# First attention: half of the mask copies moved behind v copies on VectorE, w_v loaded by column halves, output products of the early tiles one step later

## The chip, the cores and the metric

The kernel runs on one core of one Trainium2 chip. The metric is the device time of one execution in microseconds (us), lower is better. An execution is called fast when it is within 1.5% of the fastest one of its kernel; every execution quoted here was fast, except one that was run only once (its state is unknown, and it is marked).

Engines are named as in the profile: PE is TensorE's matrix unit, PEld its weight loads, DVE is VectorE, ACT is ScalarE, POOL is GpSimd, SP is SyncE (in these kernels it only issues transfers, 373 of them in the trace before). A name such as `QK<-stg` reads "output from input". `L433` is a line of the kernel before.

## The reference

Two layers, A and B, run twice in the order A, B, A, B, each added to a residual. Only the first A is touched. It is an attention over a window of 8 positions with a stride of 2:

```python
def _A_ref(x, wqkv, wo):                 # x: (1, 2048, 576), already normalized
    B, S, D = x.shape; H = 32; Dh = D // H          # 18 values per head
    W, dil = (8, 2)
    q, k, v = ...(x @ wqkv)...                      # each (B, H, S, Dh)
    idx = pos[:, None] - (jnp.arange(W) * dil)[None, :]
    mask = idx >= 0
    logits = einsum('bhsd,bhswd->bhsw', q, kg) * scale
    logits = where(mask, logits, -1e9)
    attn = softmax(logits)
    o = einsum('bhsw,bhswd->bhsd', attn, vg)
    return o.transpose(...).reshape(B, S, D) @ wo
...
x = A_x
x = x + _A_ref(_layernorm(x), A_wqkv, A_wo)
x = x + _B_ref(_layernorm(x), ...)
x = x + _A_ref(_layernorm(x), A_wqkv, A_wo)
x = x + _B_ref(_layernorm(x), ...)
```

## The kernel before

q and k of all heads lie in one tile `QK`. A head takes 18 partitions of a group of 32; the other 14 hold a pattern that adds the window mask inside the score product itself. DVE copies that pattern into `QK`, one half of the positions at a time. These are the mask copies, eight of them in two groups of four:

```python
def fill_window_rows(self, QK, half):
    ...
    c0 = PADL + half * n
    for g0 in (0, 4):
        for a in range(2):
            nc.vector.tensor_copy(out=QK[:, a, g0:g0 + 4, c0:c0 + n]...,
                                  in_=self.pat[:, a, None, None, PADL:PADL + 256].to_broadcast(...))
```

A q or k product (`PG`) is made by PE, copied to a staging tile `stg` (some staging space is borrowed from `win2a`, so the profile calls it `QK<-win2a`), and then moved into its partitions of `QK` by small transfers, issued in turn by POOL and SP:

```python
def PG(d, qk, cc, dve, queues=(nc.sync, nc.gpsimd)):
    ...
    for c in range(5):
        nc.tensor.matmul(pp[:, :], lhsT=w, rhs=self.xnT[...], start=(c == 0), stop=(c == 4))
    evac(stg[:, qk, gi * 512:(gi + 1) * 512], pp[:, :], dve)      # dve: on DVE, else on ACT
    ...
    for dst, src in moves:
        dma_rr[0] += 1
        self.dma(dst, src, eng=queues[dma_rr[0] % len(queues)])
```

The front, in its order (v products are `VW`, normalizations `R_` and `A_`):

```python
self.load_wv(nc.sync)
...
rows[1]()                       # mask rows, on DVE and POOL
setup_bufs(nc.gpsimd)
...
VW(1, 0, False)
VW(1, 1, False)
...
rows[2](nc.scalar)              # stores the mask rows, issued by ACT
...
self.fill_window_rows(QK, 0)    # first group of mask copies
...
for k_, (d, cc) in enumerate(order):
    for qk in ((1, 0) if d < 4 else (0,)):
        PG(d, qk, cc, False, ...)
    ...
    if k_ == 6:
        R_(12, 4)
        A_(12, 13, 14, 15)
        self.fill_window_rows(QK, 1)        # second group
T_(12, 13, 14, 15)
...
for t in range(nvw0, nvw):                  # v products of tiles 4 to 7
    for hh in range(2):
        VW(t, hh, False)                    # copied by ACT
```

Then come 38 steps, two for each of 19 attention tiles. A step multiplies scores (`L_ps`), takes the exponential (`P_sb`), multiplies with v (`O_ps`), writes `o_t`, and fills the rest with q, k and v products. After a tile's second step SP issues a transpose of `o_t` to `oT`, and some steps later the output product (`pw<-oT`) of a block of 128 rows uses it:

```python
for i in range(NS):
    t = -(-(i + 1) * P // QT) - 1           # last attention tile that block i needs
    s = 2 * t + (6 if li == 0 and i == 0 else 5 if t < NT - 5 else 4 if t < NT - 3 else 3)
    at(s - 5, XO, i)                        # SP loads the residual
    at(s, WO, i, 0)                         # output product, two halves
    at(s + 1, WO, i, 1)
    ...
    if i < NS - 1:
        at(s + 4, LN_T, i)                  # SP transposes the normalized rows
...
L_mm(0)
EXP(0)
for d, qk, cc in pre:                       # six more q/k products
    PG(d, qk, cc, True, q2)
for s in range(NST):
    if s + 1 < NST:
        L_mm(s + 1)
        EXP(s + 1)
    PV(s)
    for f, a in table.pop(s, []):
        f(*a)
```

The softmax here doesn't subtract the row's maximum and nothing guards it: scores larger than these inputs give would overflow.

Of the kernel before, what the change touches and what calls it, by code (L numbers as in the profile page):

```python
# [18 lines left out]
P = 128  # L19
D = 576  # L20
# [42 lines left out]
class K:  # L63
# [51 lines left out]
    def build_window_rows(self, c):  # L115
# [6 lines left out]
        nc = self.nc  # L122
        R = c.tile([P, 2, MR, 16], bf16, name="win_rows")
        self.pat = self.consts.tile([P, 2, 272], bf16, name="win_pat")
# [7 lines left out]
        nc.gpsimd.iota(n[:], pattern=[[1, 3]], base=15, channel_multiplier=1)  # L132
        nc.gpsimd.memset(R[:, 0, 0:8, :], half)
        nc.gpsimd.affine_select(out=R[:, 0, 0:8, :], in_=R[:, 0, 0:8, :], compare_op=ALU.is_ge, fill=-half,
                                base=1, pattern=[[2, 8], [-1, 16]], channel_multiplier=0)
        nc.gpsimd.memset(R[:, 1, 0:8, :], 0.0)
        for off in (2, 3):
# [152 lines left out]
            self.dma(R["wqk"][:, :, w0:w0 + n], self.A_wqkv[0:512, c0:c0 + n].rearrange("(c p) n -> p c n", p=P), eng=eng)  # L290
            self.dma(R["wqk4"][:64, w0:w0 + n], self.A_wqkv[512:576, c0:c0 + n], eng=eng)

    def load_wv(self, eng):
        R = self.right
        self.dma(R["wv"][:, 0:4, :], self.A_wqkv[0:512, 2 * D:3 * D].rearrange("(c p) n -> p c n", p=P), eng=eng)
        self.dma(R["wv"][:64, 4, :], self.A_wqkv[512:576, 2 * D:3 * D], eng=eng)

    def load_wo(self, eng):
        R = self.right
# [20 lines left out]
    def layer_A(self, li):  # L320
        nc, tc, cfg = self.nc, self.tc, self.cfg
        S, NT, XW, NS = cfg.S, cfg.NT, cfg.XW, cfg.NS
# [6 lines left out]
        QK = main.tile([P, 2, 8, XW], bf16, name="QK")  # L329
# [13 lines left out]
        R = self.right  # L343
# [7 lines left out]
        def tdim(t):  # L351
            nq = min(QT, S - QT * t)
            return HALO + nq, nq


        def setup_bufs(eng):
            for pb in P_bufs:
                eng.memset(pb[:, :, :, QT:P], 0.0)
            for ob_ in o_bufs:
                eng.memset(ob_[:, D:640], 0.0)  # L360
# [10 lines left out]
        def VW(t, hh, dve):  # L371
            nk = tdim(t)[0]
            pv = self.PT_tile([P, 512], f32, "pv")
            for c in range(5):
                nc.tensor.matmul(pv[:nk, 0:288], lhsT=self.xnT[:, c, QT * t:QT * t + nk],  # L375
                                 rhs=wv_sb[:, c, hh * 288:(hh + 1) * 288], start=(c == 0), stop=(c == 4))
            evac(v_ext[:nk, t, 16 * hh:16 * hh + 16, 0:DH], pv[:nk, 0:288].rearrange("p (b d) -> p b d", d=DH), dve)
# [4 lines left out]
        def PG(d, qk, cc, dve, queues=(nc.sync, nc.gpsimd)):  # L382

            cb, gi = divmod(cc, CBW // 512)
            key = (d, cb)
            if key not in stg_tiles:
                if cb == 0 and d >= 3 and lent:
                    stg_tiles[key] = lent[d - 3]
                else:
                    stg_tiles[key] = stgs[stg_rr[0] % NSTG]  # L390
                    stg_rr[0] += 1
                stg_left[key] = (2 if d < 4 else 1) * (CBW // 512)
            stg = stg_tiles[key]
            pp = self.PT_tile([P, 512], f32, "pp")
            w0 = d * P + (640 if qk else 0)
            for c in range(5):
                w = wqk[:, c, w0:w0 + P] if c < 4 else wqk4[:, w0:w0 + P]
                nc.tensor.matmul(pp[:, :], lhsT=w, rhs=self.xnT[:, c, PADL + cc * 512:PADL + (cc + 1) * 512],  # L398
                                 start=(c == 0), stop=(c == 4))
            evac(stg[:, qk, gi * 512:(gi + 1) * 512], pp[:, :], dve)  # L400
            stg_left[key] -= 1
            if stg_left[key] == 0:
                stg_tiles.pop(key)
                cs = slice(PADL + cb * CBW, PADL + (cb + 1) * CBW)
                moves = []
                for h in range(d * P // DH, H):
                    a, b = max(h * DH, d * P), min((h + 1) * DH, (d + 1) * P)
                    if a >= b:
                        break
                    g, rg = divmod(h, 4)  # L410
                    q0, s0, n = 32 * rg + a - h * DH, a - d * P, b - a
                    if d < 4:
                        moves.append((QK[q0:q0 + n, :, g, cs], stg[s0:s0 + n, :, :]))
                    else:
                        for a_ in range(2):
                            moves.append((QK[q0:q0 + n, a_, g, cs], stg[64 * a_ + s0:64 * a_ + s0 + n, 0, :]))
# [3 lines that stand above are left out]
# [85 lines left out]
        q2 = (nc.gpsimd, nc.sync, nc.gpsimd)  # L505


        if li == 0:
# [3 lines left out]
            def x_load(xg, i0, n, eng):  # L512
                self.dma(xg, self.A_x[i0 * P:(i0 + n) * P, :].rearrange("(i p) d -> p i d", p=P), eng=eng)
                for k_ in range(n):
                    xts[i0 + k_] = xg[:, k_, :]
# [2 lines left out]
            x_load(x0[:, 0:1, :], 0, 1, nc.sync)  # L518
            x_load(x0[:, 1:2, :], 1, 1, nc.scalar)
            x_load(x0[:, 2:4, :], 2, 2, nc.sync)  # L520
            self.load_wv(nc.sync)
            x_load(x1[:, 0:4, :], 4, 4, nc.sync)
            self.load_wqk(nc.sync)
            x_load(spare, 8, 4, nc.sync)
# [6 lines left out]
            rows = self.build_window_rows(sb)  # L531
# [5 lines left out]
            def S_(*tiles):  # L537
                for i in tiles:
                    st = sb.tile([P, 2, nc.vector.BN_STATS_DIM], f32, name="ln_st", tag="ln_st", bufs=3)
                    for s in range(2):  # L540
                        nc.vector.bn_stats(out=st[:, s, :], in_=xts[i][:, s * 288:(s + 1) * 288])
                    nc.vector.bn_aggr(out=mvs[:, i, :], in_=st[:])
# [4 lines left out]
            def R_(i0, n):  # L547
                nc.gpsimd.tensor_tensor(out=rstds[:, i0:i0 + n], in0=rstds[:, i0:i0 + n],
                                        in1=self.neg_half[:, 0:1].to_broadcast([P, n]), op=ALU.pow)
            xns = {}  # L550

            def A_(*tiles):
                for i in tiles:
                    xns[i] = xn = self.xn_bufs[self.xn_rr % len(self.xn_bufs)]
                    self.xn_rr += 1
                    nc.vector.tensor_scalar(out=xn[:, 0:D], in0=xts[i], scalar1=mvs[:, i, 0:1],
                                            scalar2=rstds[:, i:i + 1], op0=ALU.subtract, op1=ALU.mult)

            def T_pe(i):
                xn = xns.pop(i)  # L560
                pt = self.PT_tile([P, 5, P], bf16, "pt")
                for c in range(5):
                    nc.tensor.transpose(pt[:, c, :], xn[:, c * P:(c + 1) * P], self.ident[:])
                r = PADL + i * P
                nc.scalar.copy(out=self.xnT[:, :, r:r + P], in_=pt[:])  # L565
# [7 lines left out]
            S_(1)  # L573
            E_(1, 1)
            R_(1, 1)
            rows[1]()
            setup_bufs(nc.gpsimd)
            A_(0)
            T_pe(0)
            VW(0, 0, False)  # L580
            VW(0, 1, False)
            A_(1)
            T_pe(1)
            VW(1, 0, False)
            VW(1, 1, False)
            S_(2, 3)
            E_(2, 2)
            R_(2, 2)
            rows[2](nc.scalar)
            A_(2, 3)  # L590
            T_pe(2)
            T_pe(3)
            x_load(sb.tile([P, 4, D], bf16, name="x_in3", tag="x_in", bufs=2)[:], 12, 4, nc.sync)
            S_(4, 5)
            E_(4, 2)
# [23 lines left out]
            for k_, (d, cc) in enumerate(order):  # L619
                for qk in ((1, 0) if d < 4 else (0,)):  # L620
                    PG(d, qk, cc, False, (nc.gpsimd, nc.sync) if d in (0, 4) else q2)
                if k_ == 3:
                    VW(3, 0, False)
                    VW(3, 1, False)
                if k_ == 6:
                    R_(12, 4)
                    A_(12, 13, 14, 15)
                    self.fill_window_rows(QK, 1)
            T_(12, 13, 14, 15)
            nvw0, nvw = 4, 8  # L630
        else:
# [12 lines left out]
            nvw0, nvw = 0, 4  # L644
        for t in range(nvw0, nvw):
            for hh in range(2):
                VW(t, hh, False)

        pieces = []

# [18 lines left out]
                at(2 * t - 2 + hh, VW, t, hh, 2 * t - 2 + hh >= PG_END and hh == 0)  # L669
        for i in range(NS):  # L670
            t = -(-(i + 1) * P // QT) - 1
            s = 2 * t + (6 if li == 0 and i == 0 else 5 if t < NT - 5 else 4 if t < NT - 3 else 3)
            at(s - 5, XO, i)
            at(s, WO, i, 0)
            at(s + 1, WO, i, 1)
            at(s + 1, LN_STATS, i)
            at(s + 2, LN_XN, i)
            at(s + 2, XST, i)
            if i < NS - 1:
                at(s + 4, LN_T, i)  # L680
# [9 lines left out]
        L_mm(0)  # L690
        EXP(0)
        for d, qk, cc in pre:
            PG(d, qk, cc, True, q2)
        for s in range(NST):
            if s + 1 < NST:
                L_mm(s + 1)
# [343 lines left out]
```

## Time and profile before

The kernel took 1200.14 us (median of 3 executions, 1200.07 to 1201.12). One execution was profiled; its span was 1197.5 us.

| what | value | view |
|---|---|---|
| PE busy | 1182.4 us, 99% | page, part 1 |
| first attention ends (end of its last output product) | 141.93 us | trace |
| stall 1: PE waits for q and k in `QK`, until 50.9 us | 3.3 us | waits of PE |
| half clock after it | 6.8 us | windows |
| stall 2: an output product waits for a transpose, until 95.0 us | 2.0 us | waits of PE |
| half clock after it | 3.4 us | windows |

The page of the kernel before. Part 1 is the busy time of each engine, part 2 cuts the span into 40 slices of about 30 us and gives tenths, and part 4 is the chain of waits that ended last.

```profile
span 1197.5 us, 20773 instructions
...
PE 1182.4 (99%) x8554; PEld 621.5 (52%) x8554; DVE 545.3 (46%) x1200; ACT 378.1 (32%) x599; POOL 277.9 (23%) x382
...
PEclk9899999999999999999999999999999999999999
...
PE 96%; DMA 2%; ACT 1%; issue 0%; POOL 0%; SPq 0%; DVE 0%; ACTq 0%; POOLq 0%
```

PE is busy nearly always, so a change can win only where PE stands still or runs slowly. One slice, the second (30 to 60 us), has a clock digit below 9.

The waits of PE in the kernel before: what was waited for, total us, number of times, longest.

```profile
PE L_ps L433 <- DMA QK<-win2a: 3.3, 2, 3.1
...
PE pw L487 <- DMA oT<-o_t: 2.0, 1, 2.0
...
PE pv L375 <- ACT xnT L565: 1.5, 2, 0.8
```

The first line is stall 1, the second stall 2, the third a wait in the front. Next, stretches of the trace before (windows view): bounds in us, then the busy us of each engine with its number of instructions, then the granted PE clock (1.00 is full), the share of the DMA engines' time, and GB/s. A DMA share above 1 (1.19 in the first line) means that the packets' times, added up, are more than the time of the 16 engines in that stretch, so packets overlap.

```profile
47.20:50.60 3.40, 0.36 (x8) 0.26 (x8) 0.48 (x1) 0.00 (x0) 0.07 (x1) 1.00 1.19 165
...
50.60:57.40 6.80, 6.60 (x80) 2.85 (x76) 2.23 (x6) 3.45 (x4) 0.00 (x0) 0.50 0.28 86
...
90.00:95.00 5.00, 3.03 (x61) 2.12 (x57) 3.29 (x11) 3.51 (x5) 4.72 (x5) 1.00 1.18 151
95.00:98.40 3.40, 3.38 (x42) 2.09 (x43) 1.17 (x3) 1.39 (x2) 3.31 (x5) 0.50 0.97 271
```

In the 3.40 us of stall 1 PE is busy for 0.36 us. After it PE is busy (6.60 of 6.80 us) but at half its clock, and after stall 2 again, for 3.4 us. What does half a clock cost? Here is a piece of the chain of waits before (start, duration, what), first at half clock, then at full:

```profile
51.85 2.14 PE pp L398 x5
53.99 0.51 PE L_ps L433 x16
54.51 0.53 PE O_ps L453 x16
...
58.15 1.09 PE pp L398 x5
...
59.88 0.50 PE O_ps L453 x16
```

Five q/k products take twice as long, but sixteen small `O_ps` products hardly longer (0.53 against 0.50 us), and sixteen score products take 0.51 us, within the 0.33 to 0.65 us that they take at full clock. So such a stretch costs less than half of its length. By an estimate from these differences it is about 2.2 us for the 6.83 us after stall 1, and about 1.2 us for the 3.41 us after stall 2 (five output products took 1.38 us there against 0.78, five v products 1.17 against 0.63). Stall 1 thus costs about 3.3 + 2.2 us, stall 2 about 2.0 + 1.2 us. Below, a half-clock window is 3.41 us of such a stretch.

Why are q and k late? Here is the timeline before, for POOL and DVE: start, duration, engine, line, operation.

```profile
39.13 4.88 POOL L77 DMA_DIRECT2D QK<-win2a  x1
...
39.28 4.63 DVE L197 COPY QK<-win_pat 128x4096 bf16<-128x4096 bf16 x4
...
44.01 3.26 POOL L77 DMA_DIRECT2D QK<-win2a  x6
```

One issue on POOL takes 4.88 us, where its neighbours take about 0.55 us. It begins 0.15 us before the second group of mask copies and ends 0.1 us after it. Six more issues follow it. The chain of waits before, taken from 36 to 52 us, passes through these issues and the landing of one of them (start, duration, what):

```profile
44.01 2.26 POOL QK L77 x4
46.27 4.55 DMA QK<-win2a
...
50.87 0.46 PE L_ps L433 x2
```

That the copies hold the issue is read from these times: it ends 0.1 us after the copies, as the first of POOL's moves does after the first group (1.56 us, ending 0.1 us after copies from 24.0 to 28.6 us), and the semaphore that it waits for had been complete since 38.32 us, so that wait was over. In the same stretch SP issued two moves from 40.81 us on in 1.45 us.

### The profile page before, as it was taken

The page shows a single profiled execution, that of the slowest core. Times are in us where ns is not written, and L with a number is a line of the kernel's source. Part 1 is how long each engine was busy: PE and PEld are TensorE (multiplying, and loading weights), DVE is VectorE, ACT ScalarE, POOL GpSimd, SP SyncE. Part 2 cuts the span into 40 slices and gives each one's busy share as a digit, 9 for nine tenths or more (in the row PEclk, how much of TensorE's full clock was granted, in tenths as well). Part 3 has the DMA queues.
Part 4 walks back from the last instruction along what each step waited for, and adds up shares of the span by engine and source line. Part 5 has one row for each costly group of instructions (what it writes and reads, how often), then busy time and mean ns, then how long its engine had stood idle before and what let it go on. Part 6 is the DMA issues. An engine that isn't in the chain of part 4 may idle for free.

```text
span 1197.5 us, 20773 instructions
## 1 busy us (share of the span) xinstructions
PE 1182.4 (99%) x8554; PEld 621.5 (52%) x8554; DVE 545.3 (46%) x1200; ACT 378.1 (32%) x599; POOL 277.9 (23%) x382
## 2 busy tenths in 40 slices
PE   8899999999999999999999999999999999999998
PEld 5456644444444444447755775444444444444677
DVE  9577777433232232234455786763223223223311
ACT  5477677301101101101246786770110110111000
POOL 4668774100000000001144777640000000000000
PEclk9899999999999999999999999999999999999999
DMA  7679894000000000049645899900000000000332
GB/s 195 129 184 218 188 198 106 22 1 12 12 11 11 11 1 11 1 137 279 176 95 122 180 234 188 235 2 22 12 11 1 11 11 11 12 1 24 128 105 73
DMA packets 178184, 101.21 MB, mean 85 GB/s; under 512 B 135008, under 2 KB 159440, under 8 KB 178089
## 3 DMA queue, kind: packets, MB, share of 16 engines
q1 hardware_dynamic: 164792, 78.13, 30.1%
q0 software_dynamic: 6480, 15.99, 5.2%
q10 hardware_dynamic: 6816, 5.77, 1.6%
q8 instruction: 67, 1.10, 0.4%
q14 instruction: 29, 0.23, 0.1%
HBM read 42.39 MB, written 16.53 MB: 49 GB/s over the span
## 4 chain that ended last, share of the span: by engine, by line
PE 96%; DMA 2%; ACT 1%; issue 0%; POOL 0%; SPq 0%; DVE 0%; ACTq 0%; POOLq 0%
PE pg L874 42%; PE pz L856 12%; PE po L928 12%; PE pz L778 11%; PE pp L398 6%; PE pv L375 3%; PE pw L487 3%; PE O_ps L453 3%; PE L_ps L433 2%; PE pzs L778 1%; DMA QK<-win2a 1%; ACT P_sb L442 1%; DMA wv_sb<-in_A_wqkv_dram 1%; DMA oT<-o_t 0%; POOL QK L77 0%
## 5 line engine op out<-in xcount | busy, mean ns | idle before, releaser
L874 PE MATMUL pg<-Wq,Z 128*128 128x512 bf16 x2304 | 502.8, 379 | 0.0
L874 PEld LDWEIGHTS <-Z 128*128 128x128 bf16 x2304 | 225.5, 98 | 271.8
L878 DVE TENSOR_TENSOR g_tmp<-pg,ln_xn 128x512 f32<-128x512 f32 x144 | 99.6, 692 | 429.1 <-PE pg L874 429.1
L868 ACT ACTIVATE z1T<-pz 128x1024 bf16<-128x1024 f32 x72 | 73.7, 1023 | 513.9 <-PE pz L856 513.7
L77 POOL DMA_DIRECT2D wout<-in_B_w_out_dram x4 | 4.2, 1060 | 604.6 <-PE pg L874 604.6
L442 ACT ACTIVATE P_sb<-L_ps 128x896 bf16<-128x896 f32 (+1 forms) x152 | 126.7, 888 | 47.8 <-PE L_ps L433 47.3
L928 PE MATMUL po<-wout,Z 128*128 128x288 bf16 x1152 | 141.4, 286 | 0.0
L856 PE MATMUL pz<-xnT,w 128*128 128x512 bf16 (+1 forms) x640 | 136.0, 380 | 0.0
L928 PEld LDWEIGHTS <-Z 128*128 128x128 bf16 x1152 | 112.7, 98 | 28.8
L778 PEld LDWEIGHTS <-xnT 128*128 128x128 bf16 (+1 forms) x800 | 66.2, 97 | 81.0 <-issue 23.7
L778 PE MATMUL pz<-win2a,xnT 128*128 128x512 bf16 x384 | 104.8, 380 | 0.0
L879 DVE TENSOR_TENSOR Z<-g_tmp,z1T 128x512 bf16<-128x512 f32 x144 | 99.7, 692 | 9.7
L856 PEld LDWEIGHTS <-w 128*128 128x128 bf16 (+1 forms) x640 | 51.1, 97 | 80.0 <-issue 27.1
L398 PE MATMUL pp<-xnT,wqk_sb 128*128 128x512 bf16 x360 | 84.6, 385 | 0.0
L792 ACT ACTIVATE zp<-pz 128x1024 bf16<-128x1024 f32 x64 | 65.5, 1023 | 36.8 <-PE pz L778 34.2
L242 POOL TENSOR_SCALAR ln_xn<-x_new,ln_mv,ln_rstd 128x576 bf16<-128x576 f32 x32 | 73.3, 2291 | 2.8
L938 DVE TENSOR_TENSOR x_new<-po,xo 128x288 f32<-128x288 f32 (+1 forms) x64 | 28.8, 455 | 87.9 <-PE po L928 84.0
L778 PE MATMUL pz<-win2b,xnT 128*128 128x512 bf16 (+1 forms) x256 | 65.8, 380 | 0.0
L794 DVE CUSTOM_DVE_ANT_0 Z<-zp 128x1536 bf16<-128x1536 bf16 x32 | 56.3, 1760 | 15.5 <-ACT zp L792 15.4
L77 POOL DMA_DIRECT2D QK<-stg x81 | 50.3, 625 | 42.1 <-DVE stg L367 27.3
L375 PE MATMUL pv<-wv_sb,xnT 128*128 128x288 bf16 (+1 forms) x380 | 56.5, 287 | 2.3 <-ACT xnT L565 1.5
L398 PEld LDWEIGHTS <-wqk_sb 128*128 128x128 bf16 x360 | 33.5, 98 | 37.2 <-issue 2.0
(111 smaller groups left out, 893.2 us busy)
## 6 DMA issues: line engine op xcount, KB each, us to landing
xres<-x_new SPq DMA_DIRECT2D x48, 288.0 KB
xo<-xres SPq DMA_DIRECT2D x48, 288.0 KB
wout<-in_B_w_out_dram POOLq DMA_DIRECT2D x4, 1296.0 KB, 8.7
w<-in_B_w_in_dram SPq DMA_DIRECT2D x16, 256.0 KB
QK<-stg POOLq DMA_DIRECT2D x53, 72.0 KB, 4.0
QK<-stg SPq DMA_DIRECT2D x41, 72.0 KB
xo<-in_A_x_dram SPq DMA_DIRECT2D x16, 144.0 KB
win2a<-in_B_w_in_dram POOLq DMA_DIRECT2D x6, 288.0 KB, 4.4
```

The costliest lines, as they stand in the source:

```text
L242: e.tensor_scalar(out=xn[:nrows, 0:D], in0=x_t[:nrows, :], scalar1=mv[:nrows, 0:1], scalar2=rstd[:nrows, 0:1], op0=ALU.subtract, op1=ALU.mult)
L375: nc.tensor.matmul(pv[:nk, 0:288], lhsT=self.xnT[:, c, QT * t:QT * t + nk], rhs=wv_sb[:, c, hh * 288:(hh + 1) * 288], start=(c == 0), stop ...
L398: nc.tensor.matmul(pp[:, :], lhsT=w, rhs=self.xnT[:, c, PADL + cc * 512:PADL + (cc + 1) * 512], start=(c == 0), stop=(c == 4))
L442: nc.scalar.activation(out=P_bufs[(2 * s + jp) % 4][:nk, :, :, 0:nq], in_=Lv[:nk, :, :, 0:nq], func=ACT.Exp, scale=scale)
L778: nc.tensor.matmul(pzvs[ci][:, sub * 512:sub * 512 + w], lhsT=self.xnT[r0:r1, c, PADL + i * P:PADL + (i + 1) * P], rhs=win2(c)[r0:r1, c0 + ...
L792: nc.scalar.activation(out=zp[:, c0:c0 + cn], in_=pzvs[ci][:, 0:cn], func=ACT.Gelu_apprx_tanh, accum_out=sums[:, ci:ci + 1])
L856: nc.tensor.matmul(pz1s[q // 2][:, q % 2, :], lhsT=w1[r0:r1, c, sub * P:(sub + 1) * P], rhs=self.xnT[r0:r1, c, PADL + q * 512:PADL + (q + ...
L868: nc.scalar.activation(out=z1T[:, q2 * 512:(q2 + 2) * 512], in_=pz1s[q2 // 2][:, :, :].rearrange("p a b -> p (a b)"), func=ACT.Gelu_apprx_ ...
L874: nc.tensor.matmul(pg[:, :], lhsT=Z[:, jj, i, sub * P:(sub + 1) * P], rhs=Wq[q][:, i, :], start=(i == 0), stop=(i == NS - 1))
L878: nc.vector.tensor_tensor(out=tmp[:], in0=pg[:, :], in1=bsp[:, qs], op=ALU.add)
L879: nc.vector.tensor_tensor(out=uT(jj)[:, sub, qs], in0=tmp[:], in1=z1Ts[jj, sub][:, qs], op=ALU.mult)
L928: nc.tensor.matmul(acc[hh], lhsT=uT(j // 2)[:, j % 2, i * P:(i + 1) * P], rhs=wouts[j // NJH][:, j % NJH, hh * 288:(hh + 1) * 288], start= ...
```

## The change

Its intent: keep the second group of mask copies from holding POOL while POOL still has moves of q and k to issue. The normalizations of the last four blocks come one product group earlier, the eight v copies of tiles 4 to 7 go to DVE, and the mask copies stand behind them; the six q/k copies after that go to ACT. In the front, part of the mask preparation and one v product come later, and w_v comes in column halves so that the first v product need not wait for all of it. Output products of the tiles below 8 come one step later, so that their transposes have longer to land.

```diff
-    def load_wv(self, eng):
-        R = self.right
-        self.dma(R["wv"][:, 0:4, :], ...)
-        self.dma(R["wv"][:64, 4, :], ...)
+    def load_wv(self, eng, nh=1):
+        R, n = self.right, D // nh
+        for c0 in range(0, D, n):
+            cs = slice(2 * D + c0, 2 * D + c0 + n)
+            self.dma(R["wv"][:, 0:4, c0:c0 + n], ...)
+            self.dma(R["wv"][:64, 4, c0:c0 + n], ...)
...
-            self.load_wv(nc.sync)
+            self.load_wv(nc.sync, 2)
...
-            rows[1]()
-            setup_bufs(nc.gpsimd)
             A_(0)
             T_pe(0)
             VW(0, 0, False)
             VW(0, 1, False)
+            S_(2)
             A_(1)
             T_pe(1)
             VW(1, 0, False)
-            VW(1, 1, False)
-            S_(2, 3)
+            S_(3)
             E_(2, 2)
             R_(2, 2)
+            rows[1]()
+            setup_bufs(nc.gpsimd)
             rows[2](nc.scalar)
             A_(2, 3)
             T_pe(2)
             T_pe(3)
+            VW(1, 1, False)
...
-                if k_ == 6:
+                if k_ == 5:
                     R_(12, 4)
                     A_(12, 13, 14, 15)
-                    self.fill_window_rows(QK, 1)
...
         for t in range(nvw0, nvw):
             for hh in range(2):
-                VW(t, hh, False)
+                VW(t, hh, li == 0)
+        if li == 0:
+            self.fill_window_rows(QK, 1)
...
-            s = 2 * t + (6 if li == 0 and i == 0 else 5 if t < NT - 5 else 4 if t < NT - 3 else 3)
+            s = 2 * t + (6 if li == 0 and t < 8 else 5 if t < NT - 5 else 4 if t < NT - 3 else 3)
...
         for d, qk, cc in pre:
-            PG(d, qk, cc, True, q2)
+            PG(d, qk, cc, li > 0, q2)
```

Below, "the step" is the change of `s`; "the mask part" is the last four edits but that one (`k_ == 5`, the v copies on DVE, the mask copies behind them, `pre` on ACT); "the front" is the rest.

More of the change, by code (lines that the diff above doesn't have):

```diff
@@ L291, in load_wqk @@
             self.dma(R["wqk4"][:64, w0:w0 + n], self.A_wqkv[512:576, c0:c0 + n], eng=eng)
-    def load_wv(self, eng):
-        R = self.right
-        self.dma(R["wv"][:, 0:4, :], self.A_wqkv[0:512, 2 * D:3 * D].rearrange("(c p) n -> p c n", p=P), eng=eng)
-        self.dma(R["wv"][:64, 4, :], self.A_wqkv[512:576, 2 * D:3 * D], eng=eng)
+    def load_wv(self, eng, nh=1):
+        R, n = self.right, D // nh
+        for c0 in range(0, D, n):
+            cs = slice(2 * D + c0, 2 * D + c0 + n)
+            self.dma(R["wv"][:, 0:4, c0:c0 + n], self.A_wqkv[0:512, cs].rearrange("(c p) n -> p c n", p=P), eng=eng)
+            self.dma(R["wv"][:64, 4, c0:c0 + n], self.A_wqkv[512:576, cs], eng=eng)
     def load_wo(self, eng):
```

## The prediction

> **What bounds it now.** The page shows PE busy 99% of the span and 96% of the chain that ended last, so only PE's gaps and slow stretches can be won. The change touches the first attention alone. The waits view (PE) lists there: scores for `QK<-win2a` transfers 3.3 us (47.1 to 50.9, "stall 1"), an output product for the `oT<-o_t` transpose 2.0 us ("stall 2", ends 95.0), v products for xnT copies 1.5 us, for w_v 0.8 us. After both stalls the granted clock in the trace is 0.5: 6.83 us from 50.6 and 3.41 us from 95.0, costing half of that. [...] So stall 1 costs about 6.7 us, stall 2 about 3.7.
>
> **Stall 1.** Its last transfers are issued by POOL. The timeline shows POOL issuing 24 moves from 27.2 to 47.3, about 0.58 us each, except that the first took 1.56 and one took 4.88 us. These two end 0.1 us after the two groups of four mask copies on DVE (24.0 to 28.6, 39.3 to 43.9). [...]
>
> The change puts the second group behind eight v copies on DVE (0.45 us each). But its normalizations come one product group earlier, and PE still delivers the last v product near 39, so I estimate they start at 39.4 to 40.1, as before. POOL then still has about six moves to issue; one is again held 4.3 us. Last issue near 47, landing near 51: I expect stall 1 to end within 0.7 us of where it ended.
>
> **Front.** Later mask padding on POOL and tile 1's v product moved behind two transposes let PE start the q/k products about 0.6 us earlier. w_v by halves gains nothing: the xnT copy ends at 7.63, w_v lands by 7.7 to 8.0. First q/k copies on ACT save 0.3 us of PE. This only lengthens the wait in stall 1; perhaps 0.4 us survives because the first mask copies end earlier.
>
> **Stall 2.** o_t of tile 6 is ready at 85.3, but SP, issuing without a break from 78.1, sends its transpose at 90.3; landing 95.0. Output products for tiles below 8 move one step later (about 2.15 us), more than the 2.0 missing, and SP's order lets that transpose out earlier. The wait and its half clock should go: about 3.7 us. The step without an output product (103.4 to 105.7, 0.4 us wait for ACT) fills up: 0.3 us. Risk: SP stays late, and the next output product (tile 9, old distance) has little margin; I allow 0.4 us given back.
>
> **Sum.** 1200.1 − 0.4 − 3.7 − 0.3 + 0.4 ≈ 1196.1 us, range 1190.8 to 1199.6. Faster by over 2%: 0.01; within 2%: 0.98; slower by over 2%: 0.01.
>
> **To check.** Still one POOL issue of 4 to 5 us ending with the second mask group; the score wait ending near 50.5 to 51, half clock after it; no `oT<-o_t` wait near 95 and no half clock there; q/k products starting near 13.4.
>
> **What would make it wrong.** DVE reaching the copies only after POOL's last move (stall 1 gone, near 1190); a new transpose wait near 105 (gain gone, near 1199)[...].

## More of the kernel before

Why the clock falls is not shown here; only that it does, after the two stalls.

By what means a copy on DVE would hold POOL is not shown.

## The result, and the profile after

| | median us | range | executions |
|---|---|---|---|
| before | 1200.11 | 1199.36 to 1201.12 | 4 |
| after | 1194.32 | 1192.53 to 1195.31 | 4 |

A ratio in this document is the mean time of one kernel's fast runs over the mean of the other's fast runs of the same rounds, so it is not quite the ratio of the medians quoted. Here it is 0.995, with a 95% interval of 0.9932 to 0.9967: 5.8 us less by the medians, where 4.0 were predicted, and well inside the range. The change is within 2%, but it is clearly a gain.

The page of the kernel after. The profiled execution is the slowest of the four, 1195.31 us, so the two traces differ by 4.0 us and the timings by more.

```profile
span 1193.5 us, 20790 instructions
...
PE 1180.0 (99%) x8554; PEld 620.5 (52%) x8554; DVE 545.4 (46%) x1202; ACT 378.5 (32%) x597; POOL 274.3 (23%) x382
...
PEclk9999999999999999999999999999999999999999
```

No slice is below 9 in the clock any more, and PE's busy time fell by 2.4 us although it does the same 8554 products: products that no longer run at half clock fit this (by the estimate above 3.4 us before; after, one window of about 1.1 us). The last output product of the first attention ends at 137.60 us, 4.33 us earlier than before (141.93). So the first attention holds the whole difference.

The waits of PE after (the statement of `L433` stands two lines further down in the kernel after, L435):

```profile
PE pv L377 <- ACT xnT L567: 3.0, 3, 1.4
...
PE L_ps L435 <- DMA QK<-win2a: 1.9, 3, 1.0
...
PE pw L489 <- DMA oT<-o_t: 1.0, 1, 1.0
PE pw L489 <- DVE rec L461: 0.3, 1, 0.3
```

The waits of the scores (stall 1) shrank from 3.3 to 1.9 us, and the waits for transposes from 2.0 to 1.0 (plus a wait of 0.3, which the profile puts down to DVE, but which ended when tile 10's transpose had landed, at 108.84 us). In the front, the wait for `xnT` doubled. The windows after:

```profile
47.10:50.50 3.40, 1.55 (x29) 0.87 (x27) 0.00 (x0) 1.67 (x3) 0.00 (x0) 1.00 1.02 196
50.50:53.90 3.40, 3.40 (x50) 1.57 (x47) 1.41 (x3) 1.11 (x2) 0.00 (x0) 0.51 0.29 95
53.90:60.00 6.10, 6.10 (x109) 3.34 (x105) 4.17 (x9) 5.16 (x7) 2.40 (x4) 1.00 0.37 90
90.00:95.00 5.00, 5.00 (x92) 3.71 (x89) 4.02 (x12) 4.46 (x7) 4.54 (x7) 1.00 1.11 238
95.00:98.40 3.40, 3.40 (x79) 2.63 (x78) 3.02 (x10) 2.86 (x5) 3.20 (x4) 1.00 0.97 234
```

In the 3.40 us ahead of the half clock PE is now busy for 1.55 us instead of 0.36, and the half clock lasts one window of 3.4 us and not two (other traces show that this need not be the change's doing, see x1 and x2). The one at 95 us is gone: in the same 3.40 us PE now does 79 products instead of 42. The timeline after, for POOL and DVE, around the second group of mask copies:

```profile
40.88 4.62 DVE L197 COPY QK<-win_pat 128x4096 bf16<-128x4096 bf16 x4
...
41.77 1.56 POOL L77 DMA_DIRECT2D QK<-win2a  x1 [1.29 <-DMA QK<-stg]
...
43.33 1.14 POOL L77 DMA_DIRECT2D QK<-win2a  x1
...
44.45 1.15 POOL L77 DMA_DIRECT2D QK<-win2a  x1
```

The copies are still in POOL's way, but in another manner. Three issues are held, each for about one mask copy (a copy takes 1.15 us), and each ends 0.1 us after a copy ends. POOL also stood idle for 1.29 us before the first of them, until a transfer that it had issued eight issues earlier, and that used the same semaphore, had landed (at 41.48 us; the issue began at 41.77). Together the last issue ends at 46.59 us instead of 47.27, its transfer lands at 50.03, and the second scores are done at 50.30 instead of 51.32.

### The profile page after: what moved, and what is told of

Read it like the earlier page. It is cut to its first block, busy times and chain, and to the rows that moved or that the text cites. A ratio compares the mean times of both kernels' runs of the same rounds, so it can differ in the third digit from the quotient of the medians.

```text
span 1193.5 us, 20790 instructions
## 1 busy us (share of the span) xinstructions
PE 1180.0 (99%) x8554; PEld 620.5 (52%) x8554; DVE 545.4 (46%) x1202; ACT 378.5 (32%) x597; POOL 274.3 (23%) x382
## 4 chain that ended last, share of the span: by engine, by line
PE 94%; DMA 1%; ACT 0%; issue 0%; DVE 0%; DVEq 0%; ACTq 0%
PE pg L878 42%; PE pz L860 12%; PE po L932 12%; PE pz L782 11%; PE pp L400 4%; PE pw L489 3%; PE O_ps L455 3%; PE pv L377 3%; PE L_ps L435 2%; PE pzs L782 1%; ACT P_sb L444 0%; DMA QK<-win2a 0%; DMA oT<-o_t 0%; PE pt L473 0%; DVE ln_st L218 0%
## 5 line engine op out<-in xcount | busy, mean ns | idle before, releaser
L883 DVE TENSOR_TENSOR Z<-g_tmp,z1T 128x512 bf16<-128x512 f32 x144 | 99.7, 692 | 10.8 <-DVE g_tmp L882 1.4
```

Source lines behind the costliest of these rows:

```text
L883: nc.vector.tensor_tensor(out=uT(jj)[:, sub, qs], in0=tmp[:], in1=z1Ts[jj, sub][:, qs], op=ALU.mult)
```

## The experiments

Three calls, each on one chip, each with its own runs of the kernel before (11 fast ones in each).

| kernel | label | chip | median us (range) | ratio to before (95%) | first attention ends, in its trace |
|---|---|---|---|---|---|
| step alone | x1_step_alone | 4 | 1201.19 (1198.21–1203.20) | 1.0013 (0.9991–1.0034) | 140.48 |
| all but the step | x2_all_but_step | 4 | 1197.34 (1196.11–1199.98) | 0.9982 (0.9960–1.0005) | 142.07 |
| after, masks three products later | x3_masks_behind_qk | 4 | 1193.81 (1192.18–1197.82) | 0.9958 (0.9935–0.9981) | 137.67 |
| after, w_v whole | x4_wv_whole | 4 | 1194.42 (1193.31–1197.72) | 0.9960 (0.9939–0.9981) | 138.26 |
| x3, more steps, later transposes | x5_masks_step_lnt | 8 | 1194.22 (1190.52–1195.89) | 0.9947 (0.9934–0.9960) | 135.90 |
| after, later transposes | x6_lnt_later | 8 | 1193.33 (1193.12–1195.12) | 0.9947 (0.9936–0.9959) | 135.53 |
| mask part alone | x7_masks_alone | 8 | 1196.02 (1194.37–1202.11) | 0.9981 (0.9962–1.0000) | 136.94 |
| after, mask rows stored by SP | x8_rows_store_sp | 8 | 1195.35 (one run, state unknown) | none | 137.63 |
| x6, residuals in pairs | y1_lnt_later_xo_pairs | 5 | 1196.41 (1194.19–1199.02) | 0.9963 (0.9940–0.9986) | 136.34 |
| after again | y2_after_again | 5 | 1194.93 (1193.89–1196.40) | 0.9951 (0.9929–0.9972) | 137.69 |
| step alone again | y3_step_alone_again | 5 | 1199.36 (1194.77–1205.07) | 0.9987 (0.9955–1.0018) | 143.69 |
| all but the step again | y4_all_but_step_again | 5 | 1197.58 (1194.79–1201.28) | 0.9974 (0.9949–0.9998) | 136.65 |

All outputs are right. The kernel before had medians of 1199.07 (1195.18 to 1203.18), 1199.73 (1198.79 to 1202.29) and 1199.67 (1198.35 to 1206.72). The last column comes from one profiled execution each; where it and the timing disagree, as in x2, the timing is to be believed and the trace read for the mechanism only.

### Step alone, and all but the step (x1, x2; repeated as y3, y4)

x1 is the kernel before with the step:

```diff
-            s = 2 * t + (6 if li == 0 and i == 0 else 5 if ...)
+            s = 2 * t + (6 if li == 0 and t < 8 else 5 if ...)
```

> The kernel before with one line of the change: output products for tiles below 8 one step later. Theory (the step is one of two independent gains): the 2.0 us wait for the o_t transpose near 95 and the half clock after it go, stall 1 stays as before (scores released near 51, half clock 6.8 us); part is given back as a wait of about 1 us for tile 9's transpose; 1200.1 becomes 1196.5 to 1198. Rival (the whole gain of the change comes from the step): 1194 to 1195. Rival (the step only works once stall 1 is shorter): 1199 or more.

x2 is the kernel after with that line put back.

> The changed kernel without the later step. Theory: the wait for the o_t transpose near 94 is back, with half clock after it; the gain that remains is stall 1's (scores released 1 us earlier, half clock 3.4 instead of 6.8 us): 1196.5 to 1198.5. Rival (all from the step): 1199.5 to 1200.5.

The waits of PE in x1, from 20 to 142 us, and after them those of x2:

```profile
PE L_ps L433 <- DMA QK<-win2a: 3.3, 3, 2.0
...
PE pw L487 <- DMA oT<-o_t: 1.5, 2, 1.3
PE pw L487 <- issue: 1.0, 1, 1.0
```

```profile
PE pw L489 <- DMA oT<-o_t: 3.3, 1, 3.3
PE L_ps L435 <- DMA QK<-win2a: 1.9, 4, 0.8
```

In x1 stall 1 is as long as before (3.3 us; POOL is again held 4.88 us, from 39.50), and the wait at 95 us is gone with its half clock. But output products wait at 105.7 (1.03), 110.3 (0.19) and 116.0 us (1.28): 2.5 us in all, more than the 1.99 that went. The kernel was not faster: the theory's 1196.5 to 1198 missed, and 1201.19 lies where the second rival put it. In x2 stall 1 is shorter and the wait near 94 us grew from 2.0 to 3.3 us. Without the step, what is won at stall 1 runs into stall 2. The time, 1197.34, is in the theory's range.

In both traces the half clock does not follow the length of the stall. x1, with a stall 1 as long as before, has one half-clock window after it and not two: in the two times 3.41 us ahead of it PE is busy for 1.62 and 1.80 us. x2, with the shorter stall, has two windows there, and two more after stall 2 (6.83 us each time), where 3.4 was expected. Over all fourteen traces two windows follow stall 1 in the kernel before and x2, one follows in the kernel after, x1, x4, y2 and y3, and none in the other seven. So the shorter stalls tend to have fewer, but in a single pair of traces the number may be chance.

In the third call both were run again, beside the whole change:

> The changed kernel, unaltered, for a comparison of the four combinations (before, step alone, all but step, both) on one chip. Theory (the step and the rest gain together more than apart): 0.994 to 0.996 of the time before. Its trace should show the scores released between 47.9 and 50.3, and a wait for tile 9's transpose of 0.7 to 2 us.

> The kernel of x1 again. Theory (together more than apart): 0.998 to 1.002 of the time before. Rival (the parts add up, and x1 was slow by chance): 0.9965 to 0.9975.

> The kernel of x2 again. Theory: 0.9975 to 0.999 of the time before, with a wait of 2.5 us or more for tile 6's transpose in the trace. Rival (the rest alone carries the change): 0.9945 to 0.996.

The three lay where they were expected, y4 (0.9974) just outside its 0.9975. The whole change was confirmed on another chip: 0.9951. The step alone was again unresolved from 1, with single waits of up to 2.37 us at 117.9 us and three half-clock windows. Everything but the step gained 0.26%, and its trace shows the wait for the transpose at 2.67 us. The means of six runs each are 1195.01 for the whole change, 1199.80 for the step alone and 1197.82 for all but the step. So the step takes 2.8 us off when the rest is already there (the scatter of the runs puts about 2 us either way around this), while alone it took 1.2 us off in this call and added 1.6 us in the first (differences of means from the kernel before, 1201.03 and 1199.41). In this call the two parts add up to less than the whole (1.2 + 3.2 against 6.0 us); in the first, in which the whole was not run, they add up to nothing (1.6 us lost, 1.6 won). But the intervals of the ratios are too wide to exclude a plain sum. That the parts need each other is what the traces suggest; the timings alone do not prove it.

### Mask copies behind three q/k products (x3), and the mask part alone (x7)

x3 is the kernel after, with the second group of mask copies held back further, until DVE has copied three of the six q/k products of `pre`:

```diff
-        if li == 0:
-            self.fill_window_rows(QK, 1)
...
-        for d, qk, cc in pre:
-            PG(d, qk, cc, li > 0, q2)
+        for k_, (d, qk, cc) in enumerate(pre):
+            PG(d, qk, cc, li > 0 or k_ < 3, q2)
+            if li == 0 and k_ == 2:
+                self.fill_window_rows(QK, 1)
```

Its theory is that the mask copies hold POOL's issues; the words that named a mechanism for it, which no run shows, are cut.

> The changed kernel with the second group of mask copies moved again, behind the first three q/k copies of the score loop's start, which go back to VectorE; they then start near 44.9 instead of 40.9. Theory [...]: the POOL issues after 40.5, which took 1.0 to 1.6 us each, take 0.6 us; the last issue ends near 45 instead of 46.6 and the scores are released near 48.5 instead of 50.1; half clock mostly gone; 1194.1 becomes 1190.5 to 1192.5. Rival (the release is set by how long the transfers take to land, whatever DVE does): last issue and release as in the changed kernel, 1193.5 to 1194.5.

The timeline of x3 for POOL and DVE, and its waits of PE from 20 to 142 us:

```profile
43.48 1.35 POOL L77 DMA_DIRECT2D QK<-win2a  x1 [0.80 <-DMA QK<-win2a]
...
43.52 4.62 DVE L197 COPY QK<-win_pat 128x4096 bf16<-128x4096 bf16 x4
```

```profile
PE pw L489 <- DMA oT<-o_t: 3.1, 1, 3.1
...
PE L_ps L435 <- DMA QK<-win2a: 0.5, 1, 0.5
```

With the copies after nearly all of POOL's issues, only the last issue is held, for one copy. Stall 1 falls from 3.3 us (before) and 1.9 us (after) to 0.5, the scores are done at 47.15 us, and no half clock follows. In this trace the hold, the stall and its half clock shrank together.

How much of stall 1 the hold makes is still not settled. The three traces with the hold of 4.88 us (before, x1, y3) have the three latest releases of the scores, 51.3 to 51.8 us; the other eleven lie between 47.2 and 50.3. Among those eleven the holds do not decide. In x5 (below), whose copies are as late as in x3, no issue was held, POOL ended at 43.34 us, and the scores were done at 47.79 with 1.0 us of stall. In x6, on the same chip, the last four issues were held and POOL ended at 45.63 us, yet the scores were done at 47.89 with no stall. POOL's last transfer landed 4.2 us after the end of its issue in x5, and 2.0 us in x6. So the landing counts as much as the issue there, and no run takes it apart.

The time that x3's theory gave, 1190.5 to 1192.5 us, was missed. The kernel was no faster than the one with the w_v load whole on the same chip (0.9958 against 0.9960): a wait of 3.1 us for the transpose appears at 103.3 us. Two half-clock windows in the first attention, at 62.6 and 103.5 us, came with it. The first of them has no long wait ahead of it: in the windows of x3, the stretch before it shows PE busy for 2.67 of 3.40 us.

```profile
59.20:62.60 3.40, 2.67 (x66) 1.92 (x61) 1.79 (x5) 3.21 (x5) 2.13 (x4) 1.00 0.57 154
62.60:66.00 3.40, 3.40 (x39) 1.50 (x38) 1.72 (x4) 1.91 (x3) 1.34 (x3) 0.50 1.07 182
```

Such windows, which come in some executions and not in others at places like this, are a likely part of the scatter of the times; that they explain all of it was not tested.

x7 is the kernel before with the mask part alone: neither the front nor the step.

```diff
-                if k_ == 6:
+                if k_ == 5:
                     R_(12, 4)
                     A_(12, 13, 14, 15)
-                    self.fill_window_rows(QK, 1)
...
-                VW(t, hh, False)
+                VW(t, hh, li == 0)
+        if li == 0:
+            self.fill_window_rows(QK, 1)
...
-            PG(d, qk, cc, True, q2)
+            PG(d, qk, cc, li > 0, q2)
```

> The kernel before with the mask part of the change alone (v copies of tiles 4 to 7 on VectorE and the second mask group behind them, normalizations one product group earlier, first q/k copies on ScalarE), whole w_v, old front, old step. Theory: mask copies start near 40.2 (PE as before, v copies a little behind), POOL is held about a copy's length for each of three or four issues instead of once for 4.9 us; scores released near 50.3, 1 us earlier than before; the wait for tile 6's transpose grows to about 3 us and takes it back: 1199 to 1200.5, last output product of the first attention within 0.7 us of 141.9. Rival (the mask part alone is worth what it saves at the scores): 1198 or less, 140.5 or earlier.

In its trace POOL's holds are 0.77, 0.81, 1.15 and 1.15 us, the last issue ends at 45.4 us, the scores are done at 48.69 us, and no half clock follows stall 1; the transpose wait is 2.1 us, ending at 90.2, with 3.41 us of half clock after it. The theory's times missed: with a median of 1196.02 us and the end of the first attention at 136.94, the rival's values came in. The ratio 0.9981 is that of all but the step (0.9982 and 0.9974). So the mask part is enough for what the change gains without the step, and the front adds nothing that these runs resolve. Four of its runs lie between 1194.37 and 1196.21 us and two at 1200.28 and 1202.11; its trace is of the fastest.

### w_v whole (x4), and the store of the mask rows on SP (x8)

```diff
-            self.load_wv(nc.sync, 2)
+            self.load_wv(nc.sync)
```

> The changed kernel with w_v loaded whole again. Theory (two more loads shift which semaphore the ScalarE-issued store of the window rows has to wait for, so that ScalarE stands from 11.3 to 12.7 until the first piece of w_qk has landed): that store waits no longer than 11.7, the xnT copies of tiles 2 and 3 start near 11.8 instead of 12.8, the q/k products start near 13.8 instead of 14.75; the total hardly moves (1193.3 to 1194.8), since stall 1 takes it up. Rival (the halves help by landing earlier): v products of tile 0 wait for w_v again and the total is 0.5 us or more longer.

The reason for x4 was a stall in the front that had not been foreseen. Here is ACT's timeline before, and then the same after:

```profile
11.71 0.34 ACTq L77 DMA_DIRECT2D win_period<-win_rows  x1
12.09 1.29 ACT L565 COPY xnT<-pt 128x640 bf16<-128x640 bf16 x2
```

```profile
12.39 0.34 ACTq L77 DMA_DIRECT2D win_period<-win_rows  x1
12.77 1.29 ACT L567 COPY xnT<-pt 128x640 bf16<-128x640 bf16 x2 [1.43 <-DVE lnx_mv L544]
```

ACT stood for 1.43 us. The profile names DVE as the releaser, but what came between is the issue of the store on ACT's own queue. It waited for a DMA semaphore that this store shares with an earlier transfer, the first load of w_qk, and that load landed at 12.29 us in this trace (ACT's wait for the semaphore ended at 12.31, the store was issued at 12.39). The two extra issues for w_v gave the store another semaphore, but not another partner: before, too, it was that of the first load of w_qk, which landed at 11.3 us. So the theory of x4 does not hold as it stands; what differs is when that load landed. The q/k products therefore began at 14.75 us and not near 13.4 (before: 14.07).

With w_v whole, that load landed at 11.24 us, ACT was not held and the q/k products began at 13.71 us. No v product waited for w_v, so the rival falls. The time did not follow: 0.9960, against 0.9950 and 0.9951 for the change itself. The halves neither won nor lost anything that can be measured.

x8 keeps the halves and issues the store from SP:

```diff
-            rows[2](nc.scalar)
+            rows[2](nc.sync)
```

> The changed kernel, w_v still in halves, with the store of the window rows issued from the sync queue instead of ScalarE. Theory (ScalarE stood from 11.3 to 12.7 because that store waits for the semaphore of the first w_qk load): the xnT copies of tiles 2 and 3 start near 11.4 instead of 12.8 and the q/k products near 13.5 instead of 14.75, as with whole w_v (13.7). Rival (the halves delay the xnT copies by the DMA traffic itself): q/k products still near 14.7.

Its `xnT` copies were not held, and q/k products began at 13.13 us; one look gave 1195.35 us. But this does not settle how often the stall comes: x2, x3, x5, y1, y2 and y4 keep both the halves and the store on ACT, and their q/k products began at 13.2 to 13.6 us without any edit, while x6 shows 14.73. In these traces ACT waits where the w_qk load lands late (12.29 us after, 12.27 in x6) and not where it lands early (11.3 us before, 11.12 in x2). In either case PE then meets stall 1, so the front's 0.7 us are absorbed there.

### Later transposes (x5, x6, y1): what limits stall 2

The idea was that SP is busy issuing (before, from 78.13 to 90.33 us with gaps of no more than 0.12 us), so that the transpose of `o_t` is issued late because residual loads, stores and transposes of normalized rows stand ahead of it. Before, `o_t` of tile 6 was ready at 85.32 us, issued at 90.33 and landed at 94.97; after, ready at 81.80, issued at 87.12 and landed at 91.01. It was issued 5.0 and 5.3 us late. The rival reading is that the transfers themselves are the limit there, and that an earlier issue only waits longer to land.

x6 is the kernel after, with the transposes of normalized rows of six blocks two steps later; nothing needs them soon:

```diff
-                at(s + 4, LN_T, i)
+                at(s + (6 if li == 0 and i < 6 else 4), LN_T, i)
```

> The changed kernel with the first six transposes of normalized rows queued two steps later, nothing else. Theory (order in the sync queue is what makes the o_t transposes late): the o_t transposes of tiles 6 to 9 go out about 1.2 us nearer to when o_t is ready (4 us late instead of 5.2), the waits for tile 9's and tile 10's transposes (0.97 and 0.33 us) go; 1193 to 1194. Rival (landing limits): issue earlier, but landing and waits as in the changed kernel.

x5 takes this, the mask copies of x3, and the step for tiles below 12:

```diff
-            s = 2 * t + (6 if li == 0 and t < 8 else 5 if ...)
+            s = 2 * t + (6 if li == 0 and t < 12 else 5 if ...)
```

> The kernel of x3 (mask copies behind three q/k copies) with two changes for the sync queue, which in all traces so far sends the o_t transposes of tiles 6 to 11 about 5 us after o_t is ready: output products one step later for tiles below 12 instead of 8, and the first six transposes of normalized rows queued two steps later. Theory (x3's gain at the scores was given back as a 3.1 us wait for tile 9's transpose, because the sync queue stays late): that wait and the half clock after it go, the last output product of the first attention ends near 133 instead of 137.7, the time is 1189 to 1191.5, under x3, the changed kernel and the kernel before. Rival (the transposes' landing, 4 to 7 us, is the limit, whatever the order): a wait of 2 us or more is back at a later tile, last output product at 136 or later, 1193 or more.

Both traces end the first attention earlier than the change (135.53 and 135.90, against 137.60), and x6 shows no half clock at all. But both still have about 2.0 us of waits for transposes: x6 at 100.9, 105.5 and 111.1 us, x5 2.03 us in one at 114.4 with a half-clock window after it. Their ratios, both 0.9947, cannot be told from 0.9950 and 0.9951. Of the theories, that of x6 had the time right but not the waits, which did not go; that of x5 missed (1189 to 1191.5 expected). The best version is thus not better than the change by more than the scatter.

y1 clears SP's queue further: it is x6 with the residual of two blocks in one load.

```diff
+            if li == 0:
+                if i % 2 == 0:
+                    two = sb.tile([P, 2, D], x_prev_dt, name="xo", tag="xo", bufs=2)
+                    self.dma(two[:], x_prev[i * P:(i + 2) * P, :].rearrange(...), eng=nc.sync)
+                    for a in range(2):
+                        tails[i + a] = dict(xo=two[:, a, :])
+                return
```

> The kernel of x6 (changed kernel, first six transposes of normalized rows queued two steps later) with the 16 residual loads of the first attention made as 8 loads of two tiles, which takes about 0.45 us per pair off the sync queue. Theory (the sync queue's own work, not the landing of a transfer, keeps the o_t transposes late): the o_t transposes of tiles 9 to 12 go out 3 to 4 us after o_t is ready instead of about 5 (x6), no wait for an o_t transpose of over 0.5 us is left, the first attention's last output product ends 1 us or more before x6's 135.5 for the same release of the scores, the time is 1191 to 1193. Rival (landing): issue earlier, waits as in x6, 1193 to 1194.5.

It did what it was made for: transposes of tiles 7 to 11 were issued 2.2 to 3.8 us after `o_t` was ready, against 4.8 to 5.4 for tiles 6 to 11 after the change. And it did not help: they then took 5.3 to 8.8 us to land. From data ready to landing it was 9.0 to 12.1 us for these five tiles, against 8.5 to 10.8 for the same tiles after the change. Tile 10's was issued at 98.79 and landed at 107.58 us. The timeline of PE in y1 shows the wait for it (another, of 0.98 us, ended at 100.56):

```profile
107.62 0.79 PE L496 MATMUL pw<-wo_sb,oT 128*128 128x288 bf16 x5 [2.62 <-DMA oT<-o_t]
```

The ratio was 0.9963, and the theory's 1191 to 1193 us missed. So the theory that the queue's order alone makes the transposes late falls, and the rival fits. One thing is not separated: y1's residual loads are themselves larger transfers, which may have delayed the transposes behind them. The windows of y1, after those of the kernel after for the same stretches, suggest where the limit is (the last but one number is the DMA share):

```profile
75.00:90.00 15.00, 14.57 (x285) 10.19 (x285) 12.89 (x38) 11.38 (x15) 14.41 (x18) 1.00 0.97 211
90.00:100.00 10.00, 10.00 (x199) 7.46 (x197) 8.12 (x25) 8.81 (x14) 9.21 (x13) 1.00 1.17 214
100.00:110.00 10.00, 8.37 (x165) 5.70 (x162) 6.75 (x21) 7.31 (x10) 7.92 (x10) 1.00 1.14 254
```

```profile
75.00:90.00 15.00, 14.58 (x280) 10.52 (x279) 12.73 (x40) 12.18 (x17) 14.66 (x17) 1.00 1.00 200
90.00:100.00 10.00, 9.20 (x184) 6.66 (x180) 7.88 (x25) 9.30 (x13) 9.24 (x12) 1.00 1.11 239
100.00:110.00 10.00, 6.82 (x129) 4.96 (x130) 4.86 (x15) 4.95 (x8) 6.84 (x8) 1.00 1.19 212
```

The DMA share is near or above 1 from 75 us on in both (before, the share was 0.74 from 75 to 90 and 1.09 and 1.16 in the next two). In 80 to 110 us of the trace after, packets of 256 bytes, which by their number are mostly those of the transposes, make up 48% of the packets' time. That the engines' capacity is the limit is argued from these shares and from y1; no run took transfers away there.

## Why the prediction was right, and where it was not

**The total.** Predicted 1196.1 us, measured 1194.32. The range held it, and "within 2%" was right. That the sum came this near is partly luck, as the terms below show.

**Stall 1: the copies did stay in POOL's way as said, but the outcome of the move was mis-sized.** The prediction was "one is again held 4.3 us" and "I expect stall 1 to end within 0.7 us of where it ended". Its start of the mask copies (39.4 to 40.1 us) was 0.8 us too early in the first trace (40.88), because the front was late, and right in y2 (39.5). In place of one long hold, three issues were held for one copy each, POOL ended 0.68 us earlier, and the scores were released 1.02 us earlier (50.30 against 51.32). And one half-clock window followed instead of two, worth about 1.1 us by the estimate above. So this term measured about 2.1 us in the two traces, where 0.4 was allowed for stall 1 and the front together. The half-clock part of it is not shown to be the change's: x1 and y3, with the long hold, have one window too. The landing differs between executions: the same code for this stall released the scores at 47.9 to 50.3 us in the traces of the change and its variants.

**Front: wrong in the first trace, and without effect.** "Near 13.4" was predicted for the q/k products; the first trace showed 14.75, because ACT's store waited for a load through a shared semaphore, and six other traces of kernels with the same front showed 13.2 to 13.6. "w_v by halves gains nothing" held (x4). The 0.4 us for the front is not to be seen in any timing.

**Stall 2: gone as said, given back more than said.** "The wait and its half clock should go: about 3.7 us" is right in kind: the wait of 1.99 us near 95 us is gone, and so is its half clock. Together they are worth about 3.2 us, since the half clock cost about 1.2 us and not 1.7. But not both reasons given hold. SP did not let the transpose out earlier relative to its data: it was issued 5.33 us after `o_t` was ready, against 5.00. It landed earlier because its data were ready 3.5 us earlier (81.80 instead of 85.32), partly from the gain at stall 1 and partly because the step puts output products off until later; and the output product that needs it comes one step later. "I allow 0.4 us given back" was too little: waits of 0.97 us at 104.1 and 0.33 us at 108.9 came in, 1.3 us together. The 0.3 us for the step without an output product is not seen: the wait of the scores for ACT there was 0.42 us at 105.7 before and is 0.33 us at 101.6 after. The one that was named as a risk, "a new transpose wait near 105", is that wait at 104.1.

**How the terms add up in the traces.** Stall 1 and its clock about 2.1 us, stall 2 and its clock 3.2, less 1.3 given back, makes 4.0 us; the first attention ended 4.33 us earlier. (With half of the length for every half-clock stretch it would be 5.1, too much.) The prediction's 4.0 us is the same sum by luck: it had 1.7 us too little at stall 1, and against that 0.5 us too much at stall 2, 0.3 us for a step that gained nothing, and 0.9 us too little given back.

**What the prediction did not see.** It priced the step as if it stood alone. The step by itself was worth nothing that could be measured (1.0013 and 0.9987): the waits came back at tiles 9 and beyond. Beside the rest it took off 2.8 us, give or take about 2.

**What stays open.** In the kernel before, x1 and y3 the held issue began 0.1 to 0.2 us before the four mask copies and was held through all of them (4.88 us, three times the same). In y2 an issue also began 0.1 us before the group (39.4 and 39.5 us) but came free after the first copy (1.44 us). What decides between the two is not known. Nor is it known what sets off the half clock or what decides how many half-clock windows follow a stall. In the 3.40 us ahead of one PE was busy for 0.36 us (before) and 1.55 us (after), but also for 2.67 us (ending at 62.6 us in x3) and 2.72 us (ending at 68.1 us in y3), while none came after 3.41 us with 1.62 us busy (ending at 49.3 us in x1). In the kernel before PE was then busy for 6.60 of 6.80 us and the clock stayed at 0.50 throughout; after the change it rose again after 3.41 us. What makes a transpose take 3.9 us to land (tile 6 after, 4.6 before) or 8.8 us (tile 10 in y1) is not known either, nor how much of stall 1 is the hold and how much the landing. How far the two parts add up is open too, as said above.

## What to carry to other kernels

When a wait is removed from one place, look for the next consumer of the same resource before counting the gain: here much of what was won at the scores ran into transposes that did not land sooner when they were issued sooner (in y1 9.0 to 12.1 us from data ready to landing, against 8.5 to 10.8 after the change), with a DMA share of 1.00 to 1.19 from 75 to 110 us. Count an idle stretch of PE together with the half clock that follows it, and expect that to vary: here it lasted 3.41 or 6.83 us, and the same stall of 3.3 us was followed by two such windows before and by one in x1. Price such a window by the products that run in it: here five long ones took twice their time (2.14 us against 1.09), sixteen short ones hardly longer (0.53 against 0.50). Before building on a theory of queue order, issue the transfer earlier once and see whether it lands earlier.
